# Gated attention and two MoE layers on one core: moe1's weights in twelve transfers issued by ScalarE, level rows of v by way of DRAM in every segment, a new instruction order

## The chip, the cores and the metric

One core of one Trainium2 chip runs the whole program. The metric is the device time of one execution in microseconds (us). Engines are named as in the profile: PE (TensorE), DVE (VectorE), ACT (ScalarE), POOL (GpSimd), SP (SyncE, which only issues transfers); SPq and ACTq are their instruction queues.

## The reference

Three layers, one after the other, all in fp32:

```python
# 4 batches x 8 heads x 768 tokens x 48; f = sigmoid(f_logit)
for t in range(768):
    state = f[:, :, t, :, None] * state + einsum('bhd,bhe->bhde', k[:, :, t], v[:, :, t])
    y[:, :, t] = einsum('bhd,bhde->bhe', q[:, :, t], state)
x = y.transpose(0, 2, 1, 3).reshape(3072, 384)
x = ((x @ w_a) * (x @ w_b)) @ w_out                      # moe1, d_ff 1536
out = maximum(maximum(x @ w1, x @ w2), x @ w3) @ w_out2  # moe2, d_ff 768
```

## The kernel before

The 3072 tokens are worked in 12 segments (s0 to s11) of 256 tokens, three to a batch, each through attention and moe1. moe2 comes after all of them, in six blocks of 512 tokens.

**Attention of a segment.** `load_nat` brings q, k, f and v in natural layout (qn, kn, fn, vn; two transfers of 192 KB each), `load_vst` v in a second layout by eight small transfers (vst), and `load_vlev` the rows of v for three levels of the decay tree (vlev). Segments after the first write vst to a DRAM scratch (`store_vscr`) and load vlev from it by 12 transfers; segment 0 fills vlev by 28 transfers straight from vst. `direct_steps` is elementwise work on DVE, with ACT's sigmoid of f ahead of it (L228, then qn*fn at L230) and some of it on POOL. `attn_steps` turns its results on PE (L304), copies them by ACT (kt, qt, k8, k16), scales them by decay tables on DVE, and computes scores and outputs on PE. For the state it transposes kt into `w` (p_kn, L304), ACT copies that into `k64n` (c_kn, L356), and PE multiplies it with vst (p_u, L366). p_sc makes the scores, DVE masks them into `ab` (L412), p_av multiplies ab with vlev (L424). `c_out` copies the result, which SP moves into x (tile `xf`) by small transfers (x_out, L440).

**moe1 of a segment.** Every fp32 operand is split into a high and a low part that PE multiplies at its fast rate: ACT makes `xh`, DVE `xl` (L493, three each). `up` computes pa and pb (L502) for 12 columns j, two at a time; ACT copies pa (c_a), DVE multiplies by pb (v_ab, L512), ACT and DVE split the product into gh and gl (c_g L516, v_g L521), and PE adds up y (L531).

**Weights.** moe1's come in 36 tiles of 128 x 384 pairs of words, 384 KB each, in the order ua0 (three tiles), ub0, uo0, ua1, ... uo3, one transfer a tile on SP (L606 to L613). Each tile is converted by five steps: s1, two ACT operations (L573, L574); s2, a shift on DVE (L579); s3, an add on POOL; s4, a cast on ACT (L590); s5, a subtraction on DVE or POOL (L595). s4 and s5 write into the raw tile's own place. moe2's weights go through the same steps; its reused buffers (yf, yh, yl, h, osb) are old moe1 weight tiles.

**What sets the order.** Every call above is a step of a one-letter kind. The string ORDER names the kind of the next step, and instructions are issued in that order to all engines; each engine runs its own in that order. The numbers in ON_POOL say which of the freely placeable elementwise steps go to POOL instead of DVE. Kinds that matter here: `r` loads weights, `0` to `4` are s1 to s5, `c` is ACT's work in direct_steps, `d` DVE's, `P` PE's of attention, `b` ACT's of attention, `s` and `e` are xh and xl, `m` is `up`, `n` ACT's and `f` DVE's part of moe1.

**Completion counters.** The transfers that SP issues take eight counters in turn, so each transfer first waits until the one eight places before it has landed; SP waits there, with whatever stands behind.

Of the kernel before, what the change touches and what calls it, by code (L numbers as in the profile page):

```python
# [7 lines left out]
F32 = mybir.dt.float32  # L8
F32R = mybir.dt.float32r
# [15 lines left out]
    "mcmgdngmgdddmdgtdbknfqgmndPmfbbmhymdgnmdhdgbgdymdfnVmPjchgdfhghPnbmhfymhvldPhmdnhfhmdydbdhdnhhmfhnmd"
    "dddPdPhmPdfPdhmPdcbdntmyddPxdPmddfbcgxydmmbndqdymyddPdggsdfndsggsgeeyebgfdkjmnddyYmfbybdhmchgynnPhhP"
    "mdghVgdnfbmPnhfmdbhdyhdmhdhymhhnhfddmPPmnmflhPdPhvmdddndmdcyfdnmdddPmydcdfbmdtnbdPbjfPgddbmnydmdmgkc"
    "PfdhmddgdnfmymbqxmdbdyndbgdxmvfVgsdYesesyyglenfnmhdyggfmgyhPPmbyhhdPdhmgnhdhnnmhdhmfbndmfymddnhhhdct"
    "ddddmPdhPfjdcqhdynmkmPfPddnmmYhddyfPdncmbfVmddPddPddmnbbgdfxdbggdydmPxPggngyhbmmbbggyfhmnhhdhfPgvdbd"
# [48 lines left out]
def kernel(  # L78
# [488 lines left out]
    def conv_steps(kinds, units, pool_of):  # L567
# [34 lines left out]
    def raw_tile(pool, u):  # L602
        raw[u] = room(pool, u, [P, DM, 2], U32)
        return raw[u].rearrange("p c t -> p (c t)")

    def load_w1(u):  # L606
        dst = raw_tile(wp, u)
        if u[0] == "o":
            sp.dma_start(out=dst, in_=w_out[u[1] * P:(u[1] + 1) * P])
            return  # L610
        n, c, i = u
        w = {"a": w_a, "b": w_b}[n]
        sp.dma_start(out=dst, in_=w[i * P:(i + 1) * P, 2 * c * DM:2 * (c + 1) * DM])  # L613
# [91 lines left out]
    def c_down(b, t):  # L705
        osb[t] = room(wp, ("b", 2, t) if t < 3 else ("o", 6), [P, DM], F32)
# [24 lines left out]
    for u in units1():  # L731
        step("r", load_w1, u)
    conv_steps("01234", units1(), lambda u: wp)
    for s in range(NSEG):
# [3 lines left out]
        if s:  # L738
            step("V", store_vscr, s)
# [7 lines left out]
    conv_steps("ABCDE", units2, lambda u: wp if u[0] == "o" else w2p[0])  # L747
# [66 lines left out]
```

## Time and profile before

| | |
|---|---|
| median of 3 runs | 973.69 us (972.47 to 974.25) |
| the profiled execution's own time | 973.67 us |
| its span in the profile | 971.9 us, so 1.8 us lie around it |
| TensorE's mean granted clock | 0.993 |
| PE busy | 905.5 us, 93% |
| DVE, ACT, POOL busy | 59%, 35%, 31% |
| the 16 DMA engines' mean share | 27% |

Spans and starts are read in microseconds from the start of the span. A group of instructions shows its busy time, the mean of one in ns, and the idle time of its engine just before, with what ended that idle time (the releaser). PE's weight loads (PEld) lie beside its matmuls.

### The profile page before, as it was taken

What the parts mean: (1) busy time and instruction counts of PE and PEld (TensorE: products, weight loads), DVE (VectorE), ACT (ScalarE), POOL (GpSimd) and SP (SyncE); (2) the same over time, 40 slices, a digit from 0 to 9 for tenths busy, and PEclk for the clock granted to TensorE, in tenths of its full rate; (3) what the DMA queues carried; (4) which work ended last, traced back from release to release, by engine and by line L of the source; (5) the groups of instructions that cost most, each with busy time, mean ns of one, the idle gap of its engine ahead of it and who ended that gap; (6) DMA issues with size and microseconds to landing.
All of it is one profiled execution on the core that took longest, in us unless ns stands there. A gap on an engine that the chain in (4) does not pass through costs nothing.

```text
span 971.9 us, 23339 instructions
## 1 busy us (share of the span) xinstructions
PE 905.5 (93%) x9860; PEld 839.5 (86%) x9860; DVE 572.9 (59%) x893; ACT 336.1 (35%) x640; POOL 305.0 (31%) x297
## 2 busy tenths in 40 slices
PE   1348989999999999999999999999999999999998
PEld 0238879999999999999999999999888888888887
DVE  6989988978886947677865442464522232323221
ACT  3556733423333333242332323564421212112121
POOL 3533737474364336443263300362400000000000
PEclk9998989999999999999999999999999999999999
DMA  8468232334323231133321204261110110010000
GB/s 244 121 198 259 79 98 59 107 76 114 106 70 93 71 115 53 58 95 83 98 84 41 69 9 137 92 212 66 33 37 17 44 49 17 33 34 17 1 32 33
DMA packets 79184, 79.07 MB, mean 81 GB/s; under 512 B 33128, under 2 KB 69864, under 8 KB 79080
## 3 DMA queue, kind: packets, MB, share of 16 engines
q1 hardware_dynamic: 79080, 77.59, 27.1%
q8 instruction: 77, 1.26, 0.5%
q14 instruction: 27, 0.22, 0.1%
HBM read 58.48 MB, written 13.76 MB: 74 GB/s over the span
## 4 chain that ended last, share of the span: by engine, by line
PE 82%; DVE 6%; DMA 6%; SPq 3%; issue 1%; ACT 1%; POOL 0%; DVEq 0%; ACTq 0%
PE p L675 23%; PE pb L502 15%; PE y L531 14%; PE pa L502 14%; PE y L701 4%; DMA ub<-in_moe_w_b_dram 2%; PE pa L701 2%; PE pb L701 2%; DMA kn<-in_k_dram 2%; PE o L424 2%; PE w L304 2%; PE o L394 2%; SPq L440 1%; PE w L407 1%; PE w L366 1%
## 5 line engine op out<-in xcount | busy, mean ns | idle before, releaser
L502 PE MATMUL pa<-xh,ua 128*128 128x256 f32 x864 | 167.7, 290 | 0.0
L502 PE MATMUL pb<-xh,ub 128*128 128x256 f32 x864 | 166.4, 288 | 1.4 <-DVE ub L595 0.9
L531 PE MATMUL y<-gh,uo 128*128 128x256 f32 x864 | 164.7, 286 | 1.5 <-ACT gh L516 0.9
L675 PE MATMUL p<-ub,u 128*128 128x512 f32 x486 | 165.9, 395 | 0.0
L502 PEld LDWEIGHTS pa<-xh,ua 128*128 128x128 f32 x864 | 137.3, 196 | 2.2
L502 PEld LDWEIGHTS pb<-xh,ub 128*128 128x128 f32 x864 | 135.2, 192 | 4.4 <-DVE ub L595 1.3
L531 PEld LDWEIGHTS y<-gh,uo 128*128 128x128 f32 x864 | 135.9, 193 | 3.4 <-ACT gh L516 1.1
L502 PE MATMUL pa<-xl,ua 128*128 128x256 f32 x432 | 124.0, 287 | 2.1 <-DVE xl L493 2.1
L531 PE MATMUL y<-gl,uo 128*128 128x256 f32 x432 | 123.4, 286 | 2.5 <-DVE gl L521 2.5
L502 PE MATMUL pb<-xl,ub 128*128 128x256 f32 x432 | 122.5, 284 | 0.0
L675 PEld LDWEIGHTS p<-ub,u 128*128 128x128 f32 x486 | 90.5, 188 | 19.1
L675 PE MATMUL p<-ua,u 128*128 128x512 f32 x324 | 101.8, 395 | 0.0
L516 ACT CAST gh<-a 128x512 fp32r<-128x512 f32 x72 | 44.6, 620 | 139.9 <-DVE a L512 118.9
L512 DVE TENSOR_TENSOR a<-a,pb 128x512 f32<-128x512 f32 x72 | 49.1, 683 | 73.2 <-PE pb L502 71.4
L502 PEld LDWEIGHTS pa<-xl,ua 128*128 128x128 f32 x432 | 84.4, 195 | 2.8 <-DVE xl L493 2.7
L531 PEld LDWEIGHTS y<-gl,uo 128*128 128x128 f32 x432 | 83.5, 193 | 3.1 <-DVE gl L521 3.1
L685 DVE TENSOR_TENSOR uo<-uo,p 128x512 f32<-128x512 f32 x36 | 24.7, 687 | 101.1 <-PE p L675 84.0
L502 PEld LDWEIGHTS pb<-xl,ub 128*128 128x128 f32 x432 | 83.1, 192 | 0.0
L508 ACT COPY a<-pa 128x512 f32<-128x512 f32 x72 | 42.5, 590 | 88.0 <-DVE gl L521 43.9
L521 DVE TENSOR_TENSOR gl<-a,gh 128x512 fp32r<-128x512 f32 x72 | 64.1, 891 | 12.8 <-ACT gh L516 12.7
L675 PEld LDWEIGHTS p<-ua,u 128*128 128x128 f32 x324 | 60.4, 188 | 11.7
L685 DVE TENSOR_TENSOR ua<-ua,p 128x512 f32<-128x512 f32 x36 | 24.8, 688 | 72.1 <-PE p L675 72.0
(206 smaller groups left out, 1560.0 us busy)
## 6 DMA issues: line engine op xcount, KB each, us to landing
u<-in_moe_w_dram SPq DMA_DIRECT2D x18, 384.0 KB
vlev<-vscr SPq DMA_DIRECT2D x132, 48.0 KB
uo<-in_moe_w_out_dram SPq DMA_DIRECT2D x14, 384.0 KB
qn<-in_q_dram SPq DMA_DIRECT2D x24, 192.0 KB
fn<-in_f_logit_dram SPq DMA_DIRECT2D x24, 192.0 KB
kn<-in_k_dram SPq DMA_DIRECT2D x24, 192.0 KB
ua<-in_moe_w_a_dram SPq DMA_DIRECT2D x12, 384.0 KB
vn<-in_v_dram SPq DMA_DIRECT2D x24, 192.0 KB
```

The costliest lines, as they stand in the source:

```text
L304: mm(pair[0][h], lhsT=pair[1][h], rhs=ident[half(h), half(h)], is_transpose=True, start=first_of_bank(n), stop=True, skip_group_check=True)
L394: mm(os_[0][64 * hl:64 * hl + D, hi // 2, o:o + 64], lhsT=st[64 * hl:64 * hl + D, c, hi * D:hi * D + D], rhs=qv[64 * hl:64 * hl + D, hi, c ...
L424: mm(ov[64 * hl:64 * hl + D, :, 1, :], lhsT=vlev[ps, lev, g, hi * D:hi * D + D], rhs=abs_[g][ps, hi, 64 * lev:64 * lev + 64], start=False, ...
L502: mm(ps, lhsT=col(w, i, j, h), rhs=x2[x][:, i], start=(n == 0), stop=(n == 3 * KC - 1), skip_group_check=True)
L508: act.copy(out=g2[jj][0], in_=ps2["a"])
L512: vec.tensor_mul(out=a, in0=a, in1=ps2["b"])
L516: act.copy(out=g2[jj][1], in_=g2[jj][0])
L521: vec.tensor_sub(out=g2[jj][2], in0=a, in1=gh.bitcast(F32))
L531: mm(ps, lhsT=wts["o", j][:, w, m * P:m * P + P], rhs=g, start=(j == 0 and n == 0 and m != 1), stop=(j == NJ - 1 and n == 2), skip_group_c ...
L675: mm(ps, lhsT=col(n, i, f, w), rhs=y, start=(c == 0), stop=(c == 3 * KC - 1))
L685: vec.tensor_max(out=hset[k][0], in0=hset[k][0], in1=u_ps[b, f, n])
L701: mm(o_ps[t], lhsT=h[:, t * P:t * P + P], rhs=wts[down_units[f]][:, w], start=(f == 0 and n == 0), stop=(f == NF - 1 and n == 2))
```

## The change

moe1's weights are loaded by twelve transfers instead of 36: one for each of ua0, ub0, uo0, ... uo3, three tiles (1.18 MB) at a time, issued by ACT (`act.dma_start`) instead of SP. A group of three lies in one tile, and so does the converted group, in the same place. `conv_steps` does s1, s2, s3 for three tiles and then s4, s5 for the three; since the converted group takes the raw group's place, the first s4 of a group follows the third s3. ACT's and SP's transfers share the eight counters, in program order.

Segment 0 takes the way of the others for vlev: two stores of vst to DRAM and 12 loads in place of the 28 transfers.

moe2's reused buffers become slices of the group tiles (`spare`), the same sizes as before. ORDER and ON_POOL are new as a whole.

```diff
 ORDER = (
-    "zqzjckzrd0drd0vdddirdddr1tddddrddrcd0dP1drr12br2ddgd3Pgcd2b3kP4jgbd0hdgdgr13dg020dgdd4qd1ggdhbrrd01b"
+    "qzkrzzrdrj012vcdd01012t2di3ddd40103dd0d2Vdcdd3dd1dcd1ddPPbb224Pdgddbd3bgh0rdd4bdrgjd4g3gdddqgg01ddgh"
...
-                if s == 0:
-                    for x in range(64 // w):
-                        sp.dma_start(
-                            out=vlev[64 * hl + x * w:64 * hl + (x + 1) * w, lev],
-                            in_=vst[2 * x * w:2 * x * w + w, :, hl].rearrange("p g h d -> p g (h d)"),
-                        )
-                    continue
...
-        for n in range(len(units)):
-            for kind, f in zip(kinds, (s1, s2, s3, s4)):
-                step(kind, f, n)
-            flex(kinds[4], lambda e, n=n: s5(n, e))
...
-        sp.dma_start(out=dst, in_=w[i * P:(i + 1) * P, 2 * c * DM:2 * (c + 1) * DM])
+        for n0 in range(0, len(units), KC):
+            for n in range(n0, n0 + KC):
+                for kind, f in zip(kinds, (s1, s2, s3)):
+                    step(kind, f, n)
+            for n in range(n0, n0 + KC):
+                step(kinds[3], s4, n)
+                flex(kinds[4], lambda e, n=n: s5(n, e))
+
+    def load_w1(n, c):
+        g = room(wp, (n, c), [P, KC, DM, 2], U32)
+        for i in range(KC):
+            raw[("o", KC * c + i) if n == "o" else (n, c, i)] = g[:, i]
+        src = w_out[c * DM:(c + 1) * DM] if n == "o" else {"a": w_a, "b": w_b}[n][:, 2 * c * DM:2 * (c + 1) * DM]
+        act.dma_start(out=g.rearrange("p i c t -> p i (c t)"), in_=src.rearrange("(i p) c -> p i c", p=P))
+
+    def done1(u):
+        n, c, i = (u[0], u[1] // KC, u[1] % KC) if u[0] == "o" else u
+        if i == 0:
+            groups[n, c] = room(wp, (n, c), [P, KC, 2, DM], F32R)
+        return groups[n, c][:, i]
...
+    def spare(n, c, dt=F32):
+        if (n, c) not in spares:
+            spares[n, c] = room(wp, (n, c), [P, KC, 2 * DM], dt)
+        return spares[n, c]
...
-        if s:
-            step("V", store_vscr, s)
+        step("V", store_vscr, s)
```

**ACT's start.** Names in the rows: ua0, ub0, uo0 are weight groups (before, ua00 is the first tile of ua0), fn is f, cvt a scratch of the conversion; DMAHW0 to 7 are the counters. Before:

```order
L717 ACT_TABLE_LOAD
L717 ACTIVATE sc_115<-sc_115 128x1 [waits DVE_49]
L228 ACTIVATE fn_112<-fn_112 128x768 [waits DMAHW3_49,DMAHW2_49]
L573 ACTIVATE cvt_157<-ua00_154 128x384 [waits DMAHW6_49]
L574 ACTIVATE ua00_154<-ua00_154 128x384
```

In the changed kernel:

```order
L604 DMA ua0_143<-in_moe_w_a_dram 128x3x768
L729 ACT_TABLE_LOAD
L729 ACTIVATE sc_115<-sc_115 128x1 [waits DVE_49]
L604 DMA ub0_153<-in_moe_w_b_dram 128x3x768
L604 DMA uo0_156<-in_moe_w_out_dram 128x3x768 [waits DMAHW2_49]
L567 ACTIVATE cvt_160<-ua0_143 128x384 [waits DMAHW0_49]
L568 ACTIVATE ua0_143<-ua0_143 128x384
L222 ACTIVATE fn_112<-fn_112 128x768 [waits DMAHW7_49,DMAHW5_49]
```

The sigmoid of f (L228, now L222), first of ACT's work before, now stands behind three issues and the s1 of ua0's first tile, which waits for the whole group.

**ACT ahead of segment 1's k64n.** Before, the last rows ahead of it are conversions and moe1's copies:

```order
L590 CAST uo4_868<-cvt_764 128x384 [waits Pool_49]
L573 ACTIVATE cvt_871<-ua21_750 128x384 [waits DMAHW3_49,DVE_49]
L574 ACTIVATE ua21_750<-ua21_750 128x384
L516 CAST gh_885<-a_820 128x512 [waits DVE_49]
L590 CAST uo5_904<-cvt_807 128x384 [waits Pool_49]
L573 ACTIVATE cvt_909<-ua22_768 128x384 [waits DMAHW4_49,Activation_49]
L574 ACTIVATE ua22_768<-ua22_768 128x384
L356 COPY k64n_129<-w_887 128x2x8x64 [waits PE_49]
```

In the changed kernel:

```order
L604 DMA ub2_717<-in_moe_w_b_dram 128x3x768 [waits DMAHW1_49]
L584 CAST ub1_682<-cvt_638 128x384
L446 COPY k16_126<-kt_123 128x32x8
L502 COPY a_761<-pa_724 128x512 [waits PE_49]
L567 ACTIVATE cvt_774<-uo1_494 128x384 [waits DVE_49,Activation_49]
L568 ACTIVATE uo1_494<-uo1_494 128x384
L604 DMA uo2_777<-in_moe_w_out_dram 128x3x768 [waits DMAHW1_49]
L567 ACTIVATE cvt_781<-ua2_523 128x384 [waits DVE_49,Activation_49]
L568 ACTIVATE ua2_523<-ua2_523 128x384
L604 DMA ua3_785<-in_moe_w_a_dram 128x3x768 [waits DMAHW1_49]
L350 COPY k64n_129<-w_804 128x2x8x64 [waits PE_49]
```

Three weight loads now stand among ACT's last ten instructions ahead of the copy. In the program's order ub2, uo2 and ua3 are each eight transfers apart, so the second waits until ub2 has landed and the third until uo2 has.

**PE behind moe1's first four columns of segment 0.** Before, the order there is segment 1's p_od, columns 2 and 3 of pa, and then p_kn, with p_u far behind:

```order
L304 MATMUL o_683<-ident_108,op_118 128x32x2 x16
L502 MATMUL pa_875<-xh_678,ua00_225 128x256 x2
L502 MATMUL pa_875<-xl_679,ua00_225 128x256
L502 MATMUL pa_875<-xh_678,ua01_249 128x256 x2
L502 MATMUL pa_875<-xl_679,ua01_249 128x256
```

In the changed kernel:

```order
L298 MATMUL o_600<-ident_108,op_118 128x32x2 x16
L298 MATMUL w_804<-ident_108,kt_123 128x64 x16
L360 MATMUL w_830<-vst_120,k64n_129 64x48 x32
L496 MATMUL pa_873<-xh_650,ua0_191 128x256 x2
L496 MATMUL pa_873<-xl_651,ua0_191 128x256
```

p_kn (L298) and p_u (L360, which reads k64n) have moved ahead of columns 2 and 3 of pa.

## Rows read from the trace of the kernel before

**Rows 1.** The page: busy us (share of the span) and instructions of each engine.

```profile
PE 905.5 (93%) x9860; PEld 839.5 (86%) x9860; DVE 572.9 (59%) x893; ACT 336.1 (35%) x640; POOL 305.0 (31%) x297
```

**Rows 2.** Windows of PE: stretch, length, busy us (instructions), granted clock, DMA share, GB/s.

```profile
0.00:69.41 69.41, 19.01 (x405) 1.00 0.66 183
69.41:80.00 10.59, 8.34 (x46) 1.00 1.04 267
80.00:84.00 4.00, 0.72 (x9) 0.72 1.04 403
...
125.00:135.00 10.00, 6.61 (x44) 0.90 0.30 64
135.00:140.00 5.00, 5.00 (x37) 0.52 0.30 82
...
650.00:968.00 318.00, 318.00 (x1533) 1.00 0.10 34
```

**Rows 3.** Windows of all: PE, PEld, DVE, ACT, POOL busy, clock, DMA share, GB/s.

```profile
3.00:9.00 6.00, 0.00 (x0) 0.00 (x0) 0.05 (x1) 0.84 (x1) 0.00 (x0) 1.00 0.98 268
...
50.00:75.00 25.00, 10.69 (x191) 9.26 (x191) 22.36 (x45) 13.42 (x28) 9.39 (x7) 1.00 0.75 210
...
100.00:125.00 25.00, 23.06 (x392) 21.38 (x390) 25.00 (x40) 18.44 (x39) 16.10 (x12) 1.00 0.17 44
...
82.00:86.00 4.00, 2.73 (x17) 2.49 (x17) 4.00 (x8) 1.02 (x2) 1.26 (x2) 0.50 1.04 411
```

**Rows 4.** Timeline: start, us, engine, line, operation, [idle before <-releaser]; the start.

```profile
6.51 0.84 ACT L228 ACTIVATE fn<-fn 128x768 f32<-128x768 f32 x1 [4.29 <-DMA fn<-in_f_logit_dram]
...
10.00 0.96 DVE L230 TENSOR_TENSOR qn<-qn,fn 128x768 f32<-128x768 f32 x1
10.68 0.55 ACT L573 ACTIVATE cvt<-ua 128x384 f32<-128x384 f32 x1 [3.33 <-DMA ua<-in_moe_w_a_dram]
```

**Rows 5.** Groups of DVE by shape, 0 to 140 us: busy, mean ns, idle before.

```profile
L244 DVE TENSOR_TENSOR kn<-kn,fn 128x384 f32<-128x384 f32 x2 | 1.1, 547 | 0.0
L271 DVE TENSOR_TENSOR op<-op,prod 128x192 f32<-128x192 f32 x4 | 1.4, 350 | 0.0
L324 DVE TENSOR_TENSOR ft<-ft,tt 128x32 f32<-128x32 f32 x2 | 0.4, 210 | 0.0
L453 DVE TENSOR_TENSOR k<-kt,tt 128x256 f32<-128x256 f32 x2 | 0.8, 414 | 0.0
L454 DVE TENSOR_TENSOR k<-kt,gt 128x512 f32<-128x512 f32 x2 | 1.4, 680 | 0.0
L579 DVE TENSOR_SCALAR cvt<-cvt 128x384 uint32<-128x384 uint32 x36 | 14.6, 414 | 1.4 <-ACT cvt L573 1.4
```

**Rows 6.** Timeline: SP's vlev issues, p_av of segment 0, and xl to p_u.

```profile
27.69 21.03 SPq L207 DMA_DIRECT2D vlev<-vst  x28
...
51.18 2.03 PE L424 MATMUL o<-ab,vlev 64*48 64x64 f32 x45 [1.41 <-DVE ab L412]
...
73.47 0.42 DVE L493 TENSOR_TENSOR xl<-xf,xh 128x256 fp32r<-128x256 f32 x1
...
83.89 0.79 PE L502 MATMUL pa<-xh,ua 128*128 128x256 f32 x2
86.11 1.12 PE L304 MATMUL w<-ident,kt 64*128 64x64 f32 x16
88.27 1.01 ACT L356 COPY k64n<-w 128x1024 f32<-128x1024 f32 x1
91.19 1.15 PE L366 MATMUL w<-vst,k64n 64*64 64x48 f32 x64
92.32 1.45 SPq L613 DMA_DIRECT2D ub<-in_moe_w_b_dram  x3
```

**Rows 7.** Chain of waits that ended last: start, us, what.

```profile
93.34 5.26 DMA ub<-in_moe_w_b_dram
```

**Rows 8.** Waits of SP's queue, 0 to 140 us: us, count, longest.

```profile
SPq L609 <- DMA ub<-in_moe_w_b_dram: 1.3, 1, 1.3
```

More of the change, by code (lines that the diff above doesn't have):

```diff
@@ L25 @@
[L25 to L29, printed above, removed]
@@ new lines @@
+    "1b22dxPg3q0tbgksgh3gsebd14dg0rehge3mddg4mmbgdgnm140rdd02rPhPf21bhV4hPhh2n30mhjdfmh43104mh2h1nm122mcm"
+    "30f3h433140d4lh2hP04nb10yvm1202Prh1dPfm33n4412y20dPt31r4m01203fnd3my2441mf013hm22y4d0d1dn3VPfb233444"
+    "mnf01y0d10220dy3d13m443n41ym2ydmf02xn1dm2dmfx33bdmnmcdyd4PssPsf3eenbye4cmdgbf4gPdlyddmddbyddnjgmbgnm"
+    "khgndfmdmnghfnbdmyYdggdqmcdhmdfdyhdmngmPPfhddbhmynmPfgndbhddhhfyhhdmhmPhvhdnPdmddhPdPcdfmdhdtddPnydd"
+    "fmbPPbxmbcyPgdngdVdmddhqmdgxdgyfdmdbbmyggdgbdnmfnkhsgydPshehfsPeyegnjbmPfchdmhlymhdghyhnddhbmddhhtdh"
@@ new lines @@
+    "PPdnnhddvmfPPndfdmhdmymcnmdddkdPmddcdfdbndfxymYPdbbqnPgjmddbggfdVdmgnyfhdPmnmgdgydcmddfnmddbddydmfnb"
+    "mygbdgxgmmdfnyhmddgdhmfdnydmsyhsPfhnefPhybsehPehcyhmdydmvlndhhdchmnnhdPbdhkddPdhdmfmPnjPmdddfnmhdtyd"
+    "dmmfnymfdmdndydmqfcndmdymdmfPdmbnbdymPdfbddnPbmmfdgdgdPnPcgdxddmdgxgdmbfymVydbhmynmdgYfnhgdssbfjyesv"
+    "negefymyhmghdmyPldnkndndbmdgmPdhcfmhmhnfddnhhdhyhdhmfdmqdycbPhddhPhnYmdmfdddPPnhmmdfddddPmmvnfdybdPb"
+    "PdmndcmgybPfgnfPdggmdcmybndgmmdybghtdmdVghdfdnmxbymdgfsynhxhhdPdjbygsPqyfdeneselmfymgyhnhhhbhnhmdhnm"
@@ new lines @@
+    "hdmPPdmfchdndfkPPdmdhynPbdddmmddPfddnfbdPtmmdymbnbmdygfPPghymgmvbdgnfcggxgyndbmddhbmyfdmkgnfgcmdVhdP"
+    "hmdhnmyfdhxnmmjdqgymfnbPhdsssfyeeenlddfhdbhdhmdYhdymdyhmydhnnPdthnPdmhmcfdPPdnfmdnmydmfnmyYdmfhmnPdm"
+    "dvfnmymfmynmfmydmnmfnbyVdmymfdnyfmnmPddbbdPgxbmdygxldgfdssPnehegcsPcebbfyggbmymghgdydgnmhkdPnmnghbhd"
+    "fhdnmdPhdfhmmnqymmfhndbhhhyhmmYthPfVPndmjhymfPddPmddmnddyfcmhddnddPbdydmfPPbndfxmmyddnmdmfymddnmgycx"
+    "gddfgdngdmvbfysgPseggnyesemhbfydgkmdbbhddmhgynhPnPnhcmmgfbndPfmdhmyhmblhnhhmdyhfmmdhnhPPjfydmndmqhdf"
@@ new lines @@
+    "YPPdhmnmPyfdddddmnbfPcbndPbmggtxbydmfnhgdgmymfdmdydgmxndfmymdysghgsdePesngfnbbbeymVfyhmymPgddvPhnnhg"
+    "mnhmbfPmmhnfnyhhmmhhfydhhdPhndlbdddPchmPdPdhdmfPntmmdfbPPdbcmbgYnfndgbyxddmPdgmdmfygmmdddyngfgmhnVmb"
+    "dbydlgmgfbgnxfhmnymyhfnhPsPhbfysPeesehyghmhymhyhhnmbhPhnhPnmhmfnPPmhmPmfnmyfnmbmyfnxmxwfWmymnWfnmymm"
+    "WfynWmmAyBmWfnmfAnfyABBAmCmDyAEBnCWmfysCsesyeneCDfWEDYBmEyACDAmymnDnnmBECWmBfCnmmWfAEyDDAmnBfWmyBnmm"
+    "fypEWnmEGWmyWfCGnAfmHAmnCHyDDAmBWEmCGAEyWDBHfnEBfABWCCmmDWBDyCCmuAyBEnpfnEDCmuAWfmNuBAMDWCuEDWmyAMmB"
@@ new lines @@
+    "yWNnMGHEEofAnCufNADWBDWMCBEEuMBNGCDyuCyuWoYEnDDnAMAGEuNEBCoBoouAMooMuoBCNHMDEAoCuuNHBMCDouMuNNoMMDEu"
+    "MuoNpMoENoMouuMoNooGouMuoNDMMEuooNoNuMuMuoOMuOuoGGOXooONoNMoMoMuNouMNoMuMHNuuoXuNMoooHoXMuMuNMuoHXNo"
+    "MuMouoNuouoopNMuMooMuOoGNMONuoMYOOuMuNooNMouoMMuuNoNooXoMMoMooNMoGuouNuuMXoMGHHuNuoMNXXHuMoMuNooopoM"
+    "uoNoMGuoOMuOuNNMouMoMoOoOHNoMuuoGuNGuooMMuNNMuoXuMMNoNXooHHMuMXoouuMoNNouMoMoMNpuGMNooooouuHMMuoNXNO"
+    "uMMOuMXouuNOuNoMGooMuuuMOoouNNMoXMoMoNoooMuNHGuHXMouooMuNMNuoouMMoNNuooMoMooOouMNuXMXOuOuNouXMoMooNu"
@@ L565, with conv_steps @@
     NCV = 5
-    def conv_steps(kinds, units, pool_of):
+    def conv_steps(kinds, units, done):
         live = {}
@@ L588, in s4 @@
             del raw[u]
-            wts[u] = room(pool_of(u), u, [P, 2, DM], F32R)
+            wts[u] = done(u)
             act.copy(out=wts[u][:, 0], in_=t)
@@ L595, in s5 @@
             e.tensor_sub(out=w[:, 1], in0=t, in1=w[:, 0].bitcast(F32))
-        for n in range(len(units)):
-            for kind, f in zip(kinds, (s1, s2, s3, s4)):
-                step(kind, f, n)
-            flex(kinds[4], lambda e, n=n: s5(n, e))
[L602 to L612, printed above, removed]
-        sp.dma_start(out=dst, in_=w[i * P:(i + 1) * P, 2 * c * DM:2 * (c + 1) * DM])
+        for n0 in range(0, len(units), KC):
[16 more added lines that the diff above has]
+        return groups[n, c][:, i]
+    groups = {}
     def load_consts():
@@ L622, in units1 @@
             units += [(n, c, i) for n in "ab" for i in range(KC)]
-            units += [("o", 3 * c + j) for j in range(3)]
+            units += [("o", KC * c + i) for i in range(KC)]
         return units
@@ L637, in open_w2, with done2 @@
         ps_p.append(ctx.enter_context(tc.tile_pool(name="ps_p", bufs=4, space=bass.MemoryType.PSUM)))
+    def spare(n, c, dt=F32):
+        if (n, c) not in spares:
+            spares[n, c] = room(wp, (n, c), [P, KC, 2 * DM], dt)
+        return spares[n, c]
+    def done2(u):
+        if u[0] == "o":
+            return spare("o", 2, F32R)[:, u[1] % KC].rearrange("p (t c) -> p t c", t=2)
+        return room(w2p[0], u, [P, 2, DM], F32R)
     def load_w2(u):
-        pool = w2p[0]
         if u[0] == "q":
@@ L648, in load_w2 @@
             src = (w1, w2, w3)[n][i * P:(i + 1) * P, 2 * c * DM:2 * (c + 1) * DM]
-        sp.dma_start(out=raw_tile(pool, u), in_=src)
+        if u[0] == "o":
+            raw[u] = spare("b", 3)[:, u[1] % KC].bitcast(U32).rearrange("p (c t) -> p c t", t=2)
+        else:
+            raw[u] = room(w2p[0], u, [P, DM, 2], U32)
+        sp.dma_start(out=raw[u].rearrange("p c t -> p (c t)"), in_=src)
+    spares = {}
     yf, yhl, hset, o_ps, u_ps = {}, {}, {}, {}, {}
@@ L654, in load_y @@
         for i in range(KC):
-            yf[i] = room(wp, ("a", 0, i), [P, TB], F32)
+            yf[i] = spare("a", 0)[:, i, 0:TB]
             for t in range(TB // SEG):
@@ L659, in c_split_y @@
     def c_split_y(b, i):
-        us = ([("b", 0, i) for i in range(KC)], [("o", i) for i in range(KC)]) if b % 2 == 0 else \
-            ([("a", 1, i) for i in range(KC)], [("b", 1, i) for i in range(KC)])
-        yhl[b % 2, i] = [room(wp, u[i], [P, TB], F32R) for u in us]
+        yhl[b % 2, i] = [spare(*u, F32R)[:, i, 0:TB]
+                         for u in ((("b", 0), ("o", 0)) if b % 2 == 0 else (("a", 1), ("b", 1)))]
         act.copy(out=yhl[b % 2, i][0], in_=yf[i])
@@ L680, in rest2 @@
         if n == 0:
-            hset[k] = [room(wp, u, [P, TB], F32 if i == 0 else F32R) for i, u in
-                       enumerate([("o", 3 + i) if k == 0 else ("a", 2, i) for i in range(3)])]
+            h = spare(*(("o", 1), ("a", 2))[k], F32R)[:, :, 0:TB]
+            hset[k] = [spare("a", 3)[:, k, 0:TB], h[:, 0], h[:, 1]]
             act.copy(out=hset[k][0], in_=u_ps[b, f, n])
@@ L705, in c_down @@
     def c_down(b, t):
-        osb[t] = room(wp, ("b", 2, t) if t < 3 else ("o", 6), [P, DM], F32)
+        osb[t] = (spare("b", 2)[:, t] if t < KC else spare("b", 3)[:, 0])[:, 0:DM]
         act.copy(out=osb[t], in_=o_ps[t])
@@ L730 @@
     step("i", load_consts)
-    for u in units1():
-        step("r", load_w1, u)
-    conv_steps("01234", units1(), lambda u: wp)
+    for c in range(DFF // DM):
+        for n in "abo":
+            step("r", load_w1, n, c)
+    conv_steps("01234", units1(), done1)
     for s in range(NSEG):
```

28 lines of the change are left out of this document (4 added, 24 removed), and 25 rows, old and new, of the table ON_POOL.

## Prediction

> **What bounds the kernel now.** The first view is the table of busy times: PE is busy 905.5 of 971.9 us [rows 1]. Nothing in the change adds or removes a matmul, so the time moves only by what PE idles and by the clock it is granted. The windows of PE show where it idles [rows 2]: 50.4 us before its first moe1 matmul at 69.41 (19.01 busy of 69.41), 2.25 up to 80, 3.28 in 80 to 84, 3.39 in 125 to 135, nothing in the last long stretch, 650 to 968. So the forecast is made in the first 140 us. There the windows of all engines name the pacemaker: DVE is busy 22.36 of 25 us in 50 to 75, where PE does 10.69, and all of 100 to 125 [rows 3]. The start of moe1 is the end of a list on DVE, from qn*fn at 10.00 to the third xl at 73.47 + 0.42 = 73.89 [rows 4, 6]. From there PE waits once more: pa's columns 2 and 3 begin at 83.89 [rows 6], 10.0 us later. I take the change in four terms, against the profiled execution (973.67 us, against a median of 973.69, so the sum goes to either).
>
> **A, the start: +3.5 us (+1.9 to +6.4).** Before, ACT's sigmoid ran at 6.51 as soon as f was there; s1 of the first weight tile came after it, and the weights' transfers began behind the inputs [rows 4]. Now s1 of ua0/0 stands ahead of the sigmoid on ACT and needs 1.18 MB to land, and ua0 is the first transfer of all. q, k and f are also 1.18 MB, so 2.36 MB must pass. The engines moved 268 GB/s at a share of 0.98 in 3 to 9 us, so they are full there [rows 3]: 2.36 MB / 268 to 280 GB/s is 8.4 to 8.8 us, from about 2.8 us, so both land near 11.2 to 11.6 if they share evenly. s1 is two operations of 0.55 (1.05 us, they overlap a little), the sigmoid 0.84: qn*fn starts near 13.5 instead of 10.00. At best ua0 comes first (9.1) and f ends at 11: 11.9. At worst the weights' longer rows take two bytes of three and f lands at 15.4: 16.4.
>
> The Trainium skill ("DMA: Bandwidth & Descriptors", section Queues, rings and completion order) says that each of the 16 engines takes turns between the queues for which it has work, a packet at a time. By that rule alone the queue with the larger packets gets the larger part, which is the end at 16.4; the rows of before show only one data queue, so I stay with the even split.
>
> **B, DVE's list: +1.7 us (0 to +4).** From qn*fn through the third xl the order gives DVE 121 operations where it had 114. Added are three of direct_steps at 0.55, one at 0.35, three of the tables at 0.21, and of the h steps one at 0.41 and one at 0.68; dropped are a 0.35 and one s2 at 0.41 [rows 5]. 1.65 + 0.35 + 0.63 + 1.09 less 0.76 is +3.0, some +2.5 since neighbouring operations overlap a little. Against that, before DVE idled 2.64 us in 50 to 75 [rows 3], where it waited for scores and for ACT's s1; the later start can eat some of it, and I take 0.8 of it back. So xl ends at 73.9 + 3.5 + 1.7 = 79.1.
>
> Also on ACT in this stretch: ub1's load stands two rows behind ua1's and, by the counters, waits until ua1 has landed, some 6 us. Queued behind it are segment 1's sigmoid and the copies of s0's k64n. DVE reaches what these feed only about when ACT is free again, so I price it at 0; if that cover is gone it costs up to 2 us, which the upper end holds.
>
> **C, the new wait ahead of segment 1's k64n: +4.3 us (+0.7 to +5).** ACT runs ub2's load, five operations, uo2's load, two operations, ua3's load, and then k64n. uo2's issue waits until ub2 has landed, ua3's until uo2 has. Queued behind are k64n, then all of moe1's copies; and PE now wants p_u, which reads k64n, ahead of pa's columns 2 and 3. Before, SP had waits of this kind, but only small ones (1.3 us, [rows 8]), with nothing behind them but transfers. One link is the time of 1.18 MB: before, the three ub tiles were issued at 92.32 [rows 6] and the last landed at 93.34 + 5.26 = 98.60 [rows 7], 6.3 us. The lower bound is 1.18 MB at the best rate in the rows, 411 GB/s [rows 3], 2.9 us, and some 1.6 to start and land, 4.5. I take 6.3, as the same bytes in the same stretch. ub2's issue comes about 1.2 us after xl (its place in ACT's list, behind xh). Then uo2 at +6.3, ua3 at +12.6, and 0.6 for the issue, 1.01 for k64n and 1.15 for p_u [rows 6]: pa's columns 2 and 3 begin 1.2 + 12.6 + 0.6 + 2.2 = 16.6 us after xl, against 10.0 before: +6.5 (with the lower link 13.0, +3.0). p_kn and p_u are then done, 1.12 + 1.15 us that PE had to do later before; taken off, +4.3 (+0.7). PE idles 6 to 7 us in one piece there.
>
> **D, the later stalls: −2 us (−7.7 to +3).** Before, PE still idled 3.39 us in 125 to 135, and 1.94 in 100 to 125 (23.06 busy of 25 [rows 3]), and ran at a clock of 0.52 in 135 to 140, which loses 2.4 us: 7.7 in all [rows 2]. They stand where segment 2's attention on DVE is late against moe1 on PE. The order keeps the largest lead that DVE's list asks of PE there about as it was, but PE comes 9 us later to this place, and DVE, which mostly goes on through ACT's waits, gains some of that. Not all: v_ab, gh and gl stand behind ACT too. I take a quarter of the 7.7.
>
> **Priced at nothing.** The 28 vlev transfers were 21.03 us of issuing on SP from 27.69, but p_av at 51.18 waited for the mask ab, not for vlev [rows 6]; the new way (two stores, 12 loads) has the same cover, DVE's work up to the mask, and if that were gone would cost what a store and a load need to land, some 4 us. Twelve issues on ACT at some 0.6 us lie in its 65% idle time [rows 1], except the three counted. That the first s4 of a group waits for POOL's third s3 is hidden by weights that are wanted later; moe2's slices keep their sizes, and PE is busy without a gap in 650 to 968 [rows 2].
>
> **Sum.** 3.5 + 1.7 + 4.3 − 2 = +7.5: 973.7 + 7.5 = 981.2, rounded to **981**.
>
> **The rivals.**
> First, a larger loss, near 988: f lands at 15.4 (A is 6.4), and the waits on ACT starve DVE as well, so that D gives nothing back (0) and B costs 2.5: 973.7 + 6.4 + 2.5 + 5 = 987.6. For it: conversions, moe1's copies and sigmoids all stand in one order behind the waiting issue. Against it: before, DVE had work without ACT for many microseconds at a time [rows 3].
>
> Second, no change, near 974: the transfers land sooner than I think. ACT reaches each issue when its predecessor has landed, so C is 0, and A and B (1.9 + 0.1) are met by 2 of D. Against it: ub2 and uo2 have seven ACT rows between them, uo2 and ua3 two, together some 3 us of work against 4.5 at least for a link.
>
> The Trainium skill (same page, section Issuing engines are not separate DMA queues) states that transfers from several engines run on the same 16 engines and that spreading the issue saves only issue time. By that alone the move to ACT is worth nothing here, since SP's issuing is off the path, and this rival's time follows; the waits are what it leaves out.
>
> Third, the other side, faster, near 968: the stall of p_od at 80 to 84 (0.72 busy of 4 [rows 2]) and those of 105 to 137 go, because the new order has PE do segment 1's state earlier and DVE's list runs ahead while PE waits. A 1.9, B 0, C 0.7, D −7.7: −5.1, 968.6. It decides if PE has no idle piece over 0.5 us behind 100 us. For it: the order is new as a whole, and before, 7.7 us stand there to be had. Against it: it wants the good end of all four terms.
>
> That the change does not do what it says has no room here: the order shows the twelve issues on ACT.
>
> **How the numbers follow.** About 0.2%, 1.9 us, is what a measurement of this kernel can tell from no change, so no change is 971.7 to 975.6. Chances: my forecast (976 to 985.5) 0.54, the larger loss 0.18, no change 0.11, faster 0.17. That gives faster 0.17, same 0.11, slower 0.72. For 8 in 10 the range leaves out the far half of the faster case and the far half of the larger loss: 970 to 989. Slower cases alone are 976 to 990.
>
> **What would show it.** In the profile of the changed kernel: ACT's sigmoid starts near 12.5, behind s1; qn*fn starts near 13.5; the third xl ends near 79; ACT's waits name the transfers of ua1, ub2 and uo2 with 4 to 6 us each at the line of the weight loads; the copy into k64n comes some 15 us behind the third xl, with PE idle in one piece of 5 us or more just before p_u; later idle pieces of 1 to 3 us in 105 to 140. It is wrong if the loads on ACT wait less than 2 us in all, if p_u follows p_kn within 5 us, if the sigmoid starts before 9, or if idle time stands behind 200 us, which I priced at nothing.

## The result and the profile after

| | before | changed |
|---|---|---|
| median | 973.27 us (972.47 to 974.25, 4 runs) | 979.75 us (978.63 to 981.41, 4 runs) |
| ratio | | 1.0068, 95% interval 1.0047 to 1.0088 |
| span of the profiled execution | 971.9 us | 976.8 us |

The change makes the kernel 6.5 us slower; 981 (970 to 989) and slower were forecast. The two profiled executions lie 4.9 us apart (the changed kernel's is the fastest of its four), and the account below is of those 4.9.

The page of the changed kernel answers to [rows 1]; its DMA queues now are two (queue, packets, MB, share of the 16 engines):

```profile
PE 904.0 (93%) x9860; PEld 838.0 (86%) x9860; DVE 556.2 (57%) x883; ACT 334.8 (34%) x640; POOL 298.1 (31%) x307
q1 hardware_dynamic: 73920, 63.82, 22.4%
q10 hardware_dynamic: 4800, 14.16, 4.4%
```

PE's work is the same; PE idles 72.8 us (976.8 less 904.0) where it idled 66.4. The windows of PE in the changed kernel, against [rows 2] (stretch, length, busy, clock, DMA share, GB/s):

```profile
0.00:75.50 75.50, 18.55 (x404) 1.00 0.59 177
75.50:93.36 17.86, 11.52 (x134) 1.00 0.91 259
...
125.00:140.00 15.00, 13.88 (x108) 0.89 0.20 56
...
300.00:400.00 100.00, 98.92 (x1592) 1.00 0.31 84
400.00:500.00 100.00, 98.60 (x1256) 1.00 0.25 69
```

PE idles 56.95 us up to its first moe1 matmul at 75.50 (before 50.40, at 69.41), and 6.34 from there to pa's columns 2 and 3 at 93.36 (before 5.53). That is +7.4. Behind it PE idles less, 9.5 against 10.4, though 2.5 us of this are new, in 300 to 500. Over the whole span PE is busy 1.5 us less for the same matmuls, and less of the span stood at the lower granted clock (in 125 to 140 0.89, before 0.77; over the span 0.997, before 0.993). 7.4 − 0.9 − 1.5 is 5.0.

The start in the timeline, against [rows 4]:

```profile
0.73 0.42 ACTq L604 DMA_DIRECT2D ua<-in_moe_w_a_dram  x1
...
10.39 0.38 ACTq L604 DMA_DIRECT2D uo<-in_moe_w_out_dram  x1
10.81 0.55 ACT L567 ACTIVATE cvt<-ua 128x384 f32<-128x384 f32 x1 [8.12 <-DMA qn<-in_q_dram]
...
14.85 0.84 ACT L222 ACTIVATE fn<-fn 128x768 f32<-128x768 f32 x1 [3.06 <-DMA fn<-in_f_logit_dram]
15.78 1.15 DVE L224 TENSOR_TENSOR qn<-qn,fn 128x768 f32<-128x768 f32 x1 [4.04 <-DMA vn<-in_v_dram]
```

The chain of waits has ua0's transfer (start, us, what):

```profile
0.73 5.83 DMA ua<-in_moe_w_a_dram
```

ua0 landed at 6.56, q only at 10.39 and f at 14.85: qn*fn starts at 15.78, before at 10.00. In front of s1 ACT stood 8.12 us, though ua0 was there: uo0's issue waited until the second half of q had landed, by the counters that all transfers share. And the place of p_u, against [rows 6]:

```profile
81.03 0.41 DVE L487 TENSOR_TENSOR xl<-xf,xh 128x256 fp32r<-128x256 f32 x1
...
78.86 0.38 ACTq L604 DMA_DIRECT2D ub<-in_moe_w_b_dram  x1
...
84.91 0.37 ACTq L604 DMA_DIRECT2D uo<-in_moe_w_out_dram  x1
...
90.80 0.37 ACTq L604 DMA_DIRECT2D ua<-in_moe_w_a_dram  x1
91.22 1.01 ACT L350 COPY k64n<-w 128x1024 f32<-128x1024 f32 x1 [4.47 <-DMA uo<-in_moe_w_out_dram]
...
92.28 1.15 PE L360 MATMUL w<-vst,k64n 64*64 64x48 f32 x64 [2.90 <-ACT k64n L350]
```

The chain of three loads on ACT is there as forecast, its links 6.05 us (78.86 to 84.91) and 5.89 (to 90.80). PE stands 2.90 us ahead of p_u. Some matmuls are longer though the granted clock reads 1.00 in their windows: up to 86.4 a pair of matmuls with xh takes 0.63 us, as long as at a granted clock of 0.50 in 94 to 96, and later 0.40. Before, it was so in 71 to 78.

```profile
83.80 0.63 PE L496 MATMUL pb<-xh,ub 128*128 128x256 f32 x2
...
98.91 0.40 PE L496 MATMUL pb<-xh,ub 128*128 128x256 f32 x2
```

### The profile page after: what moved, and what is told of

Same layout as the page of the kernel before. It is cut to its first block, busy times and chain, and to the rows that moved or that the text cites. A ratio compares the mean times of both kernels' runs of the same rounds, so it can differ in the third digit from the quotient of the medians.

```text
span 976.8 us, 23243 instructions
## 1 busy us (share of the span) xinstructions
PE 904.0 (93%) x9860; PEld 838.0 (86%) x9860; DVE 556.2 (57%) x883; ACT 334.8 (34%) x640; POOL 298.1 (31%) x307
## 4 chain that ended last, share of the span: by engine, by line
PE 83%; DMA 5%; DVE 5%; issue 2%; ACT 2%; SPq 2%; POOL 1%; ACTq 0%; DVEq 0%
PE p L687 23%; PE pa L496 15%; PE pb L496 15%; PE y L525 14%; PE y L713 4%; PE pb L713 2%; PE pa L713 2%; PE o L418 2%; PE o L388 2%; PE w L298 2%; DMA ua<-in_moe_w_a_dram 1%; PE w L401 1%; PE w L360 1%; DMA vn<-in_v_dram 1%; PE o L298 1%
## 5 line engine op out<-in xcount | busy, mean ns | idle before, releaser
L697 DVE TENSOR_TENSOR ua<-ua,p 128x512 f32<-128x512 f32 x72 | 49.5, 687 | 147.3 <-PE p L687 141.8
L515 DVE TENSOR_TENSOR gl<-a,gh 128x512 fp32r<-128x512 f32 x72 | 61.7, 857 | 21.1 <-ACT gh L510 21.0
L687 PE MATMUL p<-uo,u 128*128 128x512 f32 x162 | 64.0, 395 | 0.0
```

Source lines behind the costliest of these rows:

```text
L515: vec.tensor_sub(out=g2[jj][2], in0=a, in1=gh.bitcast(F32))
L687: mm(ps, lhsT=col(n, i, f, w), rhs=y, start=(c == 0), stop=(c == 3 * KC - 1))
L697: vec.tensor_max(out=hset[k][0], in0=hset[k][0], in1=u_ps[b, f, n])
```

## Experiments

Two theories stood at the start: that the transfers on ACT make the loss (they share the engines with q, k and f at the start, and ACT stands behind landings later), and that the new order makes it. Both turned out too coarse. All ratios are to the kernel before, run on the same chip.

**The start alone.** Edit of the changed kernel:

```diff
-        act.dma_start(out=g.rearrange("p i c t -> p i (c t)"), in_=src...)
+        (sp if c == 0 else act).dma_start(out=g.rearrange("p i c t -> p i (c t)"), in_=src...)
-    "qzkrzzrdrj012vcdd01012t2di3ddd..."
+    "qzkzzjrvdc012dd01012trr2di3ddd..."
```

> The changed kernel, but its first three weight loads (ua0, ub0, uo0) are issued by SP: ua0 behind f's load, ub0 and uo0 behind vst's, and ACT's sigmoid stands ahead of s1 of ua0. The nine later loads stay on ACT. Theory Q (the loss begins with ua0 and ub0 taking the DMA engines from q, k and f, so that the sigmoid ran at 14.85 instead of 6.51): the sigmoid starts at 6.5 to 8, qn*fn at 9 to 10.5 instead of 15.78, the third xl 4 to 6 us earlier than 81.4, and the time falls by 4 to 6 us to 974 to 976. Theory O (the new order of DVE's, ACT's and POOL's lists makes the loss; the start is taken up by waits for the weights' conversion): the third xl moves by less than 2 us and the time stays within 978 to 981.

Measured: 979.95 us, 1.0075 (1.0056 to 1.0094), as the change, and the third xl at 80.84, 0.2 us earlier. It did not decide: the sigmoid ran at 8.17, but qn*fn at 14.58, since DVE's list has the shift of ua0's first tile ahead of it, and that tile came with its group (s1 at 13.73, behind ua0's transfer).

**The late loads alone.** All loads from ua1 on go to SP:

```diff
-        act.dma_start(...)
+        (act if c == 0 else sp).dma_start(...)
```

> The changed kernel, but the nine weight loads of ua1 to uo3 are issued by SP at the same places of the order; ua0, ub0, uo0 stay on ACT. Theory Q's second part (ACT standing behind landings keeps k64n of segment 1 from PE): ACT's wait of 4.5 us ahead of k64n is gone, PE's 2.9 us ahead of p_u with it, and the time falls by 1 to 3 us to 977 to 979. Rival (PE had other work in that stretch and what it gains there it loses in the next stall, or SP's waits now delay inputs): within 1 us of 979.75.

Measured: 980.37 us, 1.008 (1.0064 to 1.0095): no gain. PE's wait ahead of p_u shrank, by 1.8 us:

```profile
90.82 1.26 PE L360 MATMUL w<-vst,k64n 64*64 64x48 f32 x64 [1.10 <-ACT k64n L350]
```

But PE is then idle later. Windows of PE, first this kernel, then the changed one:

```profile
105.00:125.00 20.00, 17.45 (x281) 0.91 0.70 187
125.00:140.00 15.00, 13.67 (x123) 1.00 0.20 54
140.00:175.00 35.00, 32.80 (x522) 1.00 0.27 72
```

```profile
105.00:125.00 20.00, 18.10 (x312) 1.00 0.49 159
140.00:175.00 35.00, 34.85 (x586) 1.00 0.26 71
```

In 105 to 175 it idles 6.1 us where the changed kernel idles 3.2. Two things take the 1.8 us back. DVE's list had not moved: its first xl for segment 1 begins at 137.76, in the changed kernel at 137.79, and PE waits for vlev (1.47 us) and DVE on the way there. And some 2 of the 2.9 us lie in 140 to 175, where one operation on DVE takes 2.47 us instead of 0.68. First the changed kernel, then this one:

```profile
157.57 0.68 DVE L454 TENSOR_TENSOR q<-qt,ft 128x512 f32<-128x512 f32 x1
...
158.24 2.32 POOL L455 TENSOR_TENSOR kt<-qt,ft 128x1024 f32<-128x1024 f32 x1 [3.21 <-issue]
```

```profile
157.63 2.24 POOL L455 TENSOR_TENSOR kt<-qt,ft 128x1024 f32<-128x1024 f32 x1 [2.23 <-issue]
...
157.94 2.47 DVE L454 TENSOR_TENSOR q<-qt,ft 128x512 f32<-128x512 f32 x1
```

POOL began 0.31 us ahead of DVE here, and DVE's operation ends only behind POOL's. This bears on most of the runs below. In the traces of nine of the eleven kernels with the new order this operation (2.47 for 0.68) or the next on DVE (2.33 for 0.55) lies beside POOL's and is 1.8 us longer, and PE is busy 56.9 to 58.1 us in 140 to 200. The changed kernel and the order alone (below) are the two where POOL begins later and neither is long, with 59.8 and 59.9. So each of the other kernels carries about 1.8 us that its edit was not meant to bring. That POOL's operation holds up DVE's is read off these rows; it wasn't tried on its own.

**Both together.** The twelve loads on SP, and the start's order of the first run.

> Both edits together: all twelve group loads on SP, ua0 behind f, ub0 and uo0 behind vst, sigmoid ahead of s1. Theory Q: the two gains add, 972 to 975, about the kernel before (973.3). If the two places are in one chain, the second gain is swallowed by the first or the other way round: the better of the two alone. Theory O: 977 or more.

Measured: 980.24 us, 1.0083 (1.0063 to 1.0103): 977 or more, which was said for the theory of the order. It carries the long operation on DVE too; an estimate without its 1.8 us is 978.4, still far above before. ACT as the issuer isn't needed for most of the loss.

**The old way of vlev in the changed kernel.** The 28 transfers put back, segment 0's two stores taken out.

> The changed kernel with segment 0's vlev loaded as before, by 28 transfers straight from vst, in place of two stores and 12 loads. Theory Q: the vlev way is off the path, since p_av waits for the mask; within 1 us of 979.75. Rival (the way by way of DRAM delays something that the path needs, by the counters that the transfers share or by vlev itself): 2 us or more faster; or, if it was the gain of the change that hides the rest of the loss, 2 us or more slower, since SP issues for some 21 us.

Measured: 981.95 us, 1.0093 (1.0077 to 1.0108), 2.2 us above the change by the medians; the intervals overlap, and here DVE's next operation is the long one (2.33 for 0.55), so that this run doesn't price vlev's way.

**The new way of vlev in the kernel before.** The `if s == 0` branch and the condition on `store_vscr` taken out, one letter `V` put in ahead of the first `l`.

> The kernel before with segment 0's vlev by way of DRAM (two stores and 12 loads for 28 transfers), nothing else. Both theories: p_av waits for the mask, so within 1 us of before (972.5). If the kernel with the change and the old vlev way (981.95, some 2 us above the change) shows a gain of the new way that the old order has too: 970.5 to 971.5.

Measured: 971.58 us, 0.9985 (0.9976 to 0.9994): 1.2 us faster than before, the one part of the change that gains, and the fastest kernel of the study. Not by idle time: PE idles 67.0 us (969.8 less 902.8 busy), before 66.4. What fell in the profiled pair, which lies 2.1 us apart, is PE's busy time, by 2.7 us, and the granted clock was lower for a shorter time. First the kernel with the edit, then the kernel before:

```profile
80.00:95.00 15.00, 11.46 (x150) 0.89 0.77 268
125.00:140.00 15.00, 11.98 (x94) 0.89 0.35 81
```

```profile
80.00:95.00 15.00, 11.72 (x146) 0.77 0.71 254
125.00:140.00 15.00, 11.61 (x79) 0.77 0.30 70
```

Over all runs of this comparison, though, the mean granted clock is the same to 0.001 (0.9949 in the ten with the edit, 0.9943 in the twenty before), which is less than 1 us. So that the clock makes the 1.2 us is not shown; what does stays open.

**The loads of the kernel before on ACT.** `sp` to `act` in its load_w1, 36 transfers of one tile.

> The kernel before with its order, its 36 transfers of one tile issued by ACT instead of SP at the same places. The first weight load stands behind the sigmoid there, so the start isn't touched. Theory Q (ACT standing behind landings is what costs): 36 issues of about 0.4 us and waits for transfers eight places before stand in ACT's list; 2 to 6 us slower than before, 975 to 979, with ACT's waits named for weight transfers. Theory O: the waits are covered by ACT's idle time; within 1.5 us of before (972.5).

Measured: 975.87 us, 1.0034 (1.0019 to 1.0048), 3.1 us slower. ACT stands behind landings that its own work has nothing to do with:

```profile
35.13 0.55 ACT L573 ACTIVATE cvt<-uo 128x384 f32<-128x384 f32 x1 [5.73 <-DMA vlev<-vst]
...
87.71 0.55 ACT L573 ACTIVATE cvt<-ua 128x384 f32<-128x384 f32 x1 [4.49 <-DMA vlev<-vscr]
```

So with this order and 36 transfers the issuer does cost. How much is these waits and how much the 36 issues of 0.33 to 0.45 us in ACT's list (one of 1.52), the run doesn't separate.

**Inputs first.** The changed kernel, loads on ACT, letters moved at the start only: f and the sigmoid ahead of ua0, and DVE's first operations ahead of the shift.

```diff
-    "qzkrzzrdrj012vcdd01012t2di3ddd40103dd0d2V..."
+    "qzkzzjvcrrdddddr012d01012t2i3d40103dd0d2V..."
```

> The changed kernel, all loads of weights still on ACT; only letters at the start of the order are moved: q, k, f and v are issued ahead of the first weight load, the sigmoid stands ahead of it on ACT, and five of DVE's first operations stand ahead of the shifts of ua0. (With the three first loads on SP and the shifts left in place, the sigmoid had run at 8.17 but qn*fn still only at 14.58, behind the shift in DVE's list, so that run did not decide it.) Theory Q (the start makes most of the loss): qn*fn at 9 to 10.5 instead of 15.78, the third xl 3 to 5 us earlier than 81.4, time 974.5 to 977. Theory O (the new order makes it): the third xl less than 2 us earlier, or what is gained there is idle again in 95 to 205, time 978.5 or more.

Measured: 981.37 us (978.9 to 986.36), 1.0094 (1.0062 to 1.0125): no gain. Its profiled execution is the slowest of the four (986.36). There qn*fn starts 6.6 us earlier, and the gain is gone by the next wait:

```profile
9.21 0.96 DVE L224 TENSOR_TENSOR qn<-qn,fn 128x768 f32<-128x768 f32 x1 [8.35 <-ACT fn L222]
...
16.51 0.54 ACT L567 ACTIVATE cvt<-ua 128x384 f32<-128x384 f32 x1 [7.38 <-DMA vst<-in_v_dram]
...
17.09 0.36 DVE L573 TENSOR_SCALAR cvt<-cvt 128x384 uint32<-128x384 uint32 x1 [4.47 <-ACT cvt L567]
...
30.46 0.37 PE L298 MATMUL o<-ident,tp 64*128 64x64 f32 x2 [30.46 <-DVE tp L251]
```

PE's first operation stands at 30.46, in the changed kernel at 29.63, before at 19.97. DVE's list holds the shift of ua0 ahead of most of its work, and the shift waits for s1. ACT stood 7.38 us in front of s1, and the row names a transfer of vst: ahead of s1 stand the issues of ub0 (15.54) and uo0 (15.96), which by the counters wait for earlier transfers. When ua0 itself landed, no row says.

**The order alone.** The kernel before (36 tiles of their own, one transfer each on SP, vlev straight from vst) with the order of the run above and the new list of POOL's steps; two buffers of moe2 are taken a step later, so that the order fits.

> The kernel before (36 weight tiles of their own, one transfer each on SP, segment 0's vlev straight from vst), with the new order and the new list of POOL's operations, the three loads of a group at the place of the group's one, and the inputs ahead of them at the start as in the run beside it. Theory Q (transfers on ACT and in groups make the loss): 972 to 975, like the kernel before. Theory O (the order makes it): 977 to 982.

Measured: 974.34 us, 1.002 (1.0009 to 1.0031): the new order costs 1.6 us, not 6.5, though PE's first operation is 5.6 us later than before. First weight tile and first operation on PE:

```profile
10.95 0.54 ACT L574 ACTIVATE cvt<-ua 128x384 f32<-128x384 f32 x1 [1.44 <-DMA ua<-in_moe_w_a_dram]
...
25.57 0.37 PE L305 MATMUL o<-ident,tp 64*128 64x64 f32 x2 [25.57 <-DVE tp L258]
```

**The same order with tiles in groups, four ways.** One transfer a group or three of one tile, on SP or on ACT; the first cell was measured above.

```diff
-        act.dma_start(out=g.rearrange("p i c t -> p i (c t)"), in_=src...)
+        for i in range(KC):
+            sp.dma_start(out=g[:, i].rearrange("p c t -> p (c t)"), in_=src[i * P:(i + 1) * P])
```

> One of four kernels with the same order (the new one, inputs ahead at the start): the changed kernel with three transfers of one tile in place of each group's one, issued by SP. Theory G (one transfer for three tiles makes the loss, since the first shift in DVE's list waits for a whole group): about the new order alone, 973 to 975.5, first tp on PE at 25 to 26.5 instead of 30.5. Theory Q (ACT as the issuer makes it): also 973 to 975.5. Theory H (the tiles lying in groups, or the coupled conversion, make it): 979 or more.

> Same order; three transfers of one tile a group, issued by ACT. Theory G: within 1.5 us of the same on SP, 973 to 976, since a first tile lands as soon. Theory Q: 978 to 982, like the one transfer on ACT (981.37). In between (976 to 978): both, as the old order with its loads moved to ACT lost 3.1 us.

> Same order; one transfer a group, issued by SP. Theory G: 978.5 to 981.5, first tp on PE at 29 or later. Theory Q: 973 to 976.

| ratio to before | SP | ACT |
|---|---|---|
| one transfer a group | 979.27 us, 1.0065 (1.005 to 1.008) | 981.37 us, 1.0094 (1.0062 to 1.0125) |
| three of one tile | 978.51 us, 1.0052 (1.0036 to 1.0069) | 993.53 us, 1.0206 (1.0186 to 1.0226) |

Of the expectations, 978.51 falls between those of G and Q (up to 975.5) and that of H (979 or more), 979.27 is as G said, but with the first tp at 27.72 instead of 29 or later, and 993.53 is above all that were given.

On SP the size of the transfer makes no difference that the medians can tell, though in the profiled executions the third xl begins at 79.14 with one transfer a group and at 76.87 with three. With three transfers on SP the time is still 4.2 us above the order alone, with the same issuer and the same transfers. What differs is the tiles in groups with the conversion that goes with them, vlev's way and moe2's buffers. ACT's first cast of ua0, first in the order alone, then with the tiles in groups:

```profile
14.64 0.51 ACT L591 CAST ua<-cvt 128x384 fp32r<-128x384 f32 x1 [0.45 <-POOL cvt L584]
```

```profile
16.78 0.51 ACT L584 CAST ua<-cvt 128x384 fp32r<-128x384 f32 x1 [3.24 <-POOL cvt L577]
```

The cast overwrites the group, so it waits for POOL's adds of all three tiles; ACT's later work stands behind it. ACT's waits of this kind up to 140 us, before, in the order alone, and in the same order with three transfers a group on SP (us, times, longest):

```profile
ACT ub L590 <- POOL cvt L583: 3.4, 4, 1.7
ACT ua L590 <- POOL cvt L583: 3.2, 1, 3.2
ACT uo L590 <- POOL cvt L583: 2.5, 2, 1.9
```

```profile
ACT uo L591 <- POOL cvt L584: 1.7, 1, 1.7
ACT ua L591 <- POOL cvt L584: 0.4, 1, 0.4
```

```profile
ACT ua L584 <- POOL cvt L577: 5.6, 4, 3.2
ACT uo L584 <- POOL cvt L577: 4.6, 3, 2.5
ACT ub L584 <- POOL cvt L577: 4.0, 3, 2.4
```

14.2 us (as many in the changed kernel), against 2.1 in the order alone and 9.1 before, so such waits need not cost time. DVE in turn waits 3.7 us for these casts up to 140 us, in the order alone 0.7. The two kernels run 0.2 us apart up to 70 us; the third xl begins at 75.82 and 76.87, and DVE's q<-qt,tt for segment 2 at 151.37 and 153.55, 2.2 us apart. PE also waits longer for vlev of segment 1 (2.76 us at 105.46, 1.57 in the order alone), which no cast explains. Then comes the long operation on DVE (2.47 for 0.68), and the two are 4.0 us apart. In 140 to 175 PE is busy 34.82 and 32.81:

```profile
140.00:175.00 35.00, 34.82 (x593) 1.00 0.23 61
```

```profile
140.00:175.00 35.00, 32.81 (x553) 1.00 0.23 61
```

So of the 4.2 us some 1.8 are the long operation, and some 2.4 are left for the casts, vlev's way and moe2's buffers together. vlev's way gained 1.2 us on the old order, and PE has no idle time in 650 to 960 in either. What the coupled casts cost wasn't tried on its own.

**Three transfers a group in the changed kernel's own order, on ACT.**

> The changed kernel with its own order and ACT as issuer, but three transfers of one tile in place of each group's one. Theory G: the first tile of ua0 lands some 3 us sooner, but f still waits for as many bytes; the sigmoid at 12 to 15, time 976 to 979. Theory Q: 979 to 982, and ACT's waits grow with the number of transfers.

Measured: 993.67 us, 1.0213 (1.0196 to 1.023), far above both expectations. More transfers in ACT's list mean more places where it stands until the transfer eight places before has landed. In the run of the same kind with the inputs first:

```profile
102.59 1.01 ACT L350 COPY k64n<-w 128x1024 f32<-128x1024 f32 x1 [8.29 <-DMA vlev<-vscr]
...
103.66 1.96 PE L360 MATMUL w<-vst,k64n 64*64 64x48 f32 x64 [9.21 <-ACT k64n L350]
```

PE waits 9.21 us for p_u (8.99 in this run's own trace), behind transfers of vlev that k64n doesn't need. Of ACT as the issuer, one transfer a group is the cheap form in this order.

## Why the prediction was right, and where it was not

**The frame held.** PE's work stayed, and the time moved by what PE idles, nearly all of it up to p_u. The direction was right and the size near (981 for 979.75), the size in part by luck: of the four terms A came out 2.3 above its figure and C 4.7 below, and D met its figure only with a loss that was priced at nothing. The terms as measured, 5.8 + 1.8 − 0.4 − 2.4, give 4.8 of the 4.9 us between the profiled executions.

**A was mis-sized:** +5.8 for +3.5, near its upper end of 6.4. The even split of the engines was the step that failed: ACT's queue had landed ua0's 1.18 MB at 6.56, while SP's first 0.39 MB, q, took until 10.39, and f landed at 14.85, near the 15.4 of the uneven split. By the Trainium skill's rule of turns between queues, a packet at a time ("DMA: Bandwidth & Descriptors", section Queues, rings and completion order), the queue with the larger packets would get the larger part, and the trace agrees in the direction: 8.3 us lie between the landings of the first 1.18 MB of the two queues. That the engines were full at 268 GB/s did not hold either: in the same 3 to 9 us the changed kernel moved 352 GB/s, at a share of 1.03. A's mechanism was only half of it. s1 ran at 10.81 because of uo0's issue ahead of it, not for ua0; and that the sigmoid stood behind s1 cost nothing, since f was later still. With the inputs first the time stayed, because DVE's shift waits for s1, and s1 stood behind the issues of ub0 and uo0 there.

**B's number held:** the third xl begins at 81.03 instead of 73.47, 7.6 late; less A's 5.8 that leaves 1.8, forecast 1.7. That it is the nine added operations is not shown: PE's first operation, which waits for DVE's tp, is already 9.7 late (29.63 for 19.97), so DVE fell further back early and made some of it up. ACT's wait for ua1 ahead of ub1 (5.87 us in the trace) was priced at nothing, with k64n of segment 0 behind it. PE's wait for that k64n was 3.20 us in the changed kernel and 3.21 in the order alone, whose loads are on SP, so that price held.

**C was mis-sized:** −0.4 for +4.3, below its range of 0.7 to 5. From the end of the third xl to pa's columns 2 and 3 it is 11.9 us, for 10.0 before, and the 2.27 of work done early come off. (16.6 less 10.0 is 6.6, not the 6.5 of the working; the 4.3 is right.) The links were right (6.05 and 5.89 for 6.3), the place was not: ub2 was issued at 78.86, 2.6 us ahead of the end of the third xl and not 1.2 behind it, and PE had moe1's first columns to do up to 87.33, as the rows above show in the long form of the matmul. So k64n came 9.8 us behind the end of the third xl and not some 15, PE idled 2.9 in place of 6 to 7, and p_u began 3.6 us behind p_kn, within the 5 that were named as a sign of being wrong. Taking the loads off ACT gave 1.8 of these back, and nothing of the time.

**D's number held, by two errors:** −2.4, forecast −2, is what all that lies behind 93.36 comes to, 0.9 of idle and 1.5 of busy time. In D's own stretch PE idles 3.0 us up to 140 where it idled 5.3, and if the 1.5 belongs there too that is some −3.8, half of the 7.7 and not a quarter. Behind it 1.4 us of idle went in other places, and idle time came behind 200 us, which was priced at nothing and named as a sign of being wrong: 2.8 us in 205 to 600, at columns that wait for ACT's and DVE's copies. The order alone has the same kind (2.8 us in that stretch), so it is the order's.

**Priced at nothing:** vlev's way gained 1.2 us on the old order, though PE's idle time did not fall there; by what stays open. That the first cast of a group waits for POOL's third add was called hidden by weights that are wanted later. It isn't hidden from ACT and DVE: 14.2 us of ACT's waits and 3.7 of DVE's lie up to 140 us in the run with three transfers on SP. What of it reaches the time is part of some 2.4 us and not known apart.

**The rival of no change** had the Trainium skill's rule beside it that issuing from several engines saves only issue time ("DMA: Bandwidth & Descriptors", section Issuing engines are not separate DMA queues). No run here agrees with that as the whole price: the old order with its loads on ACT lost 3.1 us, with ACT standing in its own list until earlier transfers had landed.

**The account by runs:** the order 1.6 us; the tiles in groups with their casts, vlev's way and moe2's buffers some 2.4. The rest of the 6.5, some 2.5, is not pinned: between one transfer and three on SP, and between one transfer a group on SP and on ACT, the intervals overlap.

## What to carry to other kernels

An in-order engine pays for a wait whether or not the waiting step is urgent. Before a buffer is shared by several steps, or a transfer is issued from a compute engine, look at what stands behind it in that engine's list. A stall that is removed need not give its time back: here DVE's list, which had not moved, had taken back the 1.8 us won at p_u within 50 us. Compare also how long the same operation takes in two kernels, not only how long engines wait: an operation on DVE that lay beside POOL's in one kernel and not in the other hid as much as the parts under study. And move the parts of a change one at a time: one of them gained 1.2 us under the others' loss.

## What the runs showed of the hardware that was not expected

Two queues with equal bytes did not land together: the first 1.18 MB on ACT's queue, in rows of 3 KB, landed at 6.56 us, the first 1.18 MB on SP's, in rows of 1.5 KB, at 14.85. And a transfer issued on one queue waits for the landing of one on the other through the shared counters: three transfers a group on ACT cost 15.0 us more than on SP (993.53 against 978.51), one a group 2.1 more, within the intervals.

One operation on DVE took 2.47 us instead of 0.68 when POOL's multiplication from the same two tiles had begun 0.28 to 0.32 us ahead of it (five kernels), and the next one 2.33 instead of 0.55 when POOL's began 0.26 to 0.3 behind the first (four kernels). In the two kernels where POOL's began 0.67 us behind the first, both took their usual time.
